# A routed expert layer on six PSUM banks instead of three, with its evictions 384 wide, its weight splitting one step apart, and two conversion pieces moved into the delta rule

## The chip, the core and the metric

The kernel runs on one core of one Trainium2 chip. The core has a matrix engine (TensorE, "PE" in the profile; its weight loads are "PEld"), three engines for the work around it (VectorE "DVE", ScalarE "ACT", GpSimd "POOL"), and queues of transfers that SyncE ("SP") and POOL issue. Matmul results land in PSUM, of which this program names eight banks. The metric is the device time of one launch in microseconds; lower is better.

## The reference

Three stages, each feeding the next:

```python
# 1 delta rule: 4 batches x 8 heads, 768 steps, head size 48
for t in range(S):
    y[:, :, t] = q_t @ state
    state = state + beta_t * outer(k_t, v_t - state.T @ k_t)     # k normalised
# 2 experts: 3072 tokens of 384 features, 8 experts of 1024
expert_idx = argmax(normalised(x) @ normalised(expert_emb).T / tau)
out[mask] = gate_w[mask, None] * (maximum(x[mask] @ w1[e], 0) @ w2[e])
# 3 second network, 384 -> 2048 -> 384; its weights arrive as float64
h = maximum(x @ w_in, 0);  return (h * h) @ w_out
```

## The kernel before

**Arithmetic.** The experts and the second network compute each fp32 product in three matmuls on halves of the numbers (`mm3`, L1136 to L1139): high x high, high x low, low x high. So every weight and every activation exists as a high part (a rounded copy, made by ACT) and a low part (the number less its high part, made by DVE, which must read the high part).

**Stages.** First the delta rule, in 24 steps of 32 tokens (s = 0 to 23), on PE, ACT and DVE in turn; then the experts, one after the other (`moe`, the loop over `e`); then the second network in eight blocks of 384 tokens.

**One expert.** The first layer is eight blocks (`fb`) of nine matmuls, each block into one PSUM bank, taken in turn from a list of three (`P1`: SP_1, YP, GP0). A block is evicted three times: ACT writes the high part `hh` with a Relu (L1234, 448 tokens), DVE the low part `hl` (L1235, 448 tokens), and ACT the 64 tokens past 384 once more, unsplit, as `ht` (L1238, into the tile `lb`). Then the rows of the next expert are transposed on three other banks (`PT`: CH0, CH1, SP_0) and split by `split_x` (ACT L966, DVE L967). Then comes the second layer, in parts t = 0, 3, 1, 2 of 128 tokens, of which part 3 is the tail of 64. `by_count` chooses on the device by the real count of tokens: blocks of 448 with a tail, or blocks of 384 without. In these runs experts 0, 3, 6 and 7 are of the first kind ("full"), 1, 2, 4 and 5 of the second ("short"); the evictions are 448 wide for both.

**Work around the matmuls.** Tables inside `run(k)` place it: k = 1 to 8 stands behind the eight blocks, k = 9 to 12 behind the four parts of the second layer. Two kinds are placed so.

`weights(upto)` splits weight pieces of 768 columns, eight for an expert: ACT copies the high part (L576), DVE subtracts for the low part (L579). The first four are this expert's second layer, loaded by `load_w2` into the tiles `hb` and `lb` (L1131). The other four are the next expert's first layer; they come through a ring of three slots, and `fetch` (L609) asks for piece n+2 when piece n is split.

`q64` is the conversion of the second network's float64 weights to float32 on their raw words: 24 pieces of six DVE operations (L1085, L1089, L1103, L1093, L1105, L1097) and an absolute value on ACT, in place (L1094). The buffers `t4k` of the raw words are two; the load of the next piece (L1069) is issued on SP at the start of each piece. The float32 result goes to DRAM (`wscr`), written by POOL. Nineteen of the DVE operations are placed in an expert, fifteen of them behind the second layer's first three parts.

All of an engine's instructions run in the order of the program, so on ACT and DVE a placed operation stands between two evictions, and an eviction waits until the operations ahead of it are done.

## Time and profile before

| quantity | value |
|---|---|
| median of three runs | 955.38 us (950.41, 955.38, 956.13) |
| profiled execution | 947.13 us, of it 945.4 us span |
| mean granted TensorE clock | 0.968 of full |
| busy over the span | PE 874.5 us (92%), DVE 601.5 (64%), ACT 446.6 (47%), POOL 101.4 (11%) |
| delta rule | to 264.90 us, the first expert matmul |
| experts | 264.90 to 529.65 us |
| second network | from 536.62 us |

Busy shares are means over stages with different limits. A row of the timeline gives start, duration, engine, line and operation, tile written <- tiles read, and in brackets how long the engine stood idle ahead of it and what ended that. The ends of matmuls are modelled and overlap, so their cadence is read from start to start. Lines are those of the kernel before.

### The profile page before, as it was taken

How to read it: one execution, taken by the hardware profiler on the slowest of the kernel's cores; microseconds unless marked ns; L12 is line 12 of the kernel's file. 1: busy time of each engine (PE TensorE's matmuls, PEld its weight loads, DVE VectorE, ACT ScalarE, POOL GpSimd, SP SyncE). 2: the span in 40 equal slices, each digit the busy share in tenths (PEclk: the TensorE clock that was granted, in tenths of full speed). 3: DMA queues.
4: the chain of work that ended last, by engine and by line, in shares of the span. 5: the costliest groups of instructions: out<-in, count | busy, mean ns of one | idle time of the engine just before them, and what ended most of it. 6: DMA issues, size and time to landing. Idle time of an engine off the chain costs nothing.

```text
span 945.4 us, 21992 instructions
## 1 busy us (share of the span) xinstructions
PE 874.5 (92%) x8859; PEld 791.9 (84%) x8859; DVE 601.5 (64%) x1478; ACT 446.6 (47%) x1074; POOL 101.4 (11%) x140
## 2 busy tenths in 40 slices
PE   4678889999899988998999899999999999999998
PEld 2456666767688877888887899999999999999998
DVE  6999999997668777777877781616243342526150
ACT  2256777778644554554455571515142333324140
POOL 3002011213102112212211200000000000000000
PEclk7599999999899999999999999999999999999999
DMA  8685876132256676658536640101010202020000
GB/s 332 231 264 201 255 200 185 41 143 81 71 140 202 227 245 212 229 175 285 188 132 235 200 116 30 22 17 34 17 34 11 40 9 42 10 42 1 26 1 25
DMA packets 103551, 117.13 MB, mean 124 GB/s; under 512 B 60339, under 2 KB 82202, under 8 KB 103440
## 3 DMA queue, kind: packets, MB, share of 16 engines
q1 hardware_dynamic: 95056, 88.72, 30.8%
q0 software_dynamic: 8224, 26.87, 7.6%
q8 instruction: 75, 1.23, 0.6%
q14 instruction: 36, 0.29, 0.1%
q10 hardware_dynamic: 160, 0.01, 0.0%
HBM read 83.47 MB, written 32.89 MB: 123 GB/s over the span
## 4 chain that ended last, share of the span: by engine, by line
PE 48%; DVE 4%; issue 3%; DMA 3%; ACT 2%; SPq 0%; POOL 0%; DVEq 0%; ACTq 0%; POOLq 0%
PE gp L1137 6%; PE gp L1138 6%; PE gp L1139 6%; PE xp L1137 4%; PE xp L1138 4%; PE xp L1139 4%; PE sp L1137 3%; PE yp L1138 3%; PE yp L1137 3%; PE sp L1138 3%; PE yp L1139 3%; PE sp L1139 3%; DMA W<-in_moe_w_dram 1%; DMA x<-y,rows 1%; DVE hl L1235 1%
## 5 line engine op out<-in xcount | busy, mean ns | idle before, releaser
L1339 DVE TENSOR_TENSOR t4k<-t2k 128x384 f32<-128x384 f32 x128 | 71.3, 557 | 200.4 <-ACT t2k L1338 197.9
L1137 PE MATMUL xp<-wb,hh 128*128 128x384 f32 x184 | 62.5, 340 | 0.0
L1138 PE MATMUL xp<-wb,hh 128*128 128x384 f32 x184 | 62.2, 338 | 0.0
L1139 PE MATMUL xp<-wb,hl 128*128 128x384 f32 x184 | 62.1, 338 | 0.0
L272 DVE TENSOR_TENSOR TL<-TL,tmp 128x135 f32<-128x135 f32 (+15 forms) x186 | 60.8, 337 | 1.8
L264 DVE TENSOR_TENSOR tmp<-AL,TL 128x135 f32<-128x135 f32 (+15 forms) x186 | 60.6, 337 | 1.6
L1137 PE MATMUL sp<-xh,W 128*128 128x384 f32 (+1 forms) x156 | 53.9, 345 | 6.2 <-ACT lb L1238 6.0
L1283 POOL DMA_INDIRECT x<-y,rows x32 | 37.8, 1181 | 160.6 <-ACT y L1280 91.8
L1138 PE MATMUL sp<-xl,W 128*128 128x384 f32 (+1 forms) x156 | 53.3, 341 | 0.2 <-DVE xl L967 0.2
L1137 PE MATMUL yp<-xh,W 128*128 128x384 f32 (+1 forms) x156 | 53.4, 342 | 0.0
L1138 PE MATMUL yp<-xl,W 128*128 128x384 f32 (+1 forms) x156 | 53.3, 342 | 0.0
L1139 PE MATMUL sp<-xh,W 128*128 128x384 f32 (+1 forms) x156 | 53.3, 342 | 0.0
L1139 PE MATMUL yp<-xh,W 128*128 128x384 f32 (+1 forms) x156 | 53.3, 342 | 0.0
L1137 PE MATMUL gp<-wb,hh 128*128 128x384 f32 x152 | 51.7, 340 | 0.0
L1138 PE MATMUL gp<-wb,hh 128*128 128x384 f32 x152 | 51.3, 338 | 0.0
L1139 PE MATMUL gp<-wb,hl 128*128 128x384 f32 x152 | 51.3, 338 | 0.0
L1137 PE MATMUL gp<-xh,W 128*128 128x384 f32 (+1 forms) x144 | 49.0, 340 | 1.2 <-ACT lb L1238 1.2
L367 ACT ACTIVATE Sb<-sp 48x384 f32<-48x384 f32 x92 | 44.6, 484 | 9.9 <-PE sp L357 8.7
L1139 PE MATMUL gp<-xh,W 128*128 128x384 f32 (+1 forms) x144 | 48.8, 339 | 0.0
L1138 PE MATMUL gp<-xl,W 128*128 128x384 f32 (+1 forms) x144 | 48.8, 339 | 0.0
L1362 ACT ACTIVATE y<-gp 128x384 f32<-128x384 f32 x12 | 5.9, 492 | 84.3 <-PE gp L1139 84.3
L357 PE MATMUL sp<-Wb,kL 128*48 128x96 f32 x736 | 42.4, 259 | 2.3 <-DVE Wb L319 1.1
(328 smaller groups left out, 2433.8 us busy)
## 6 DMA issues: line engine op xcount, KB each, us to landing
hb<-in_moe_w_dram SPq DMA_DIRECT2D x24, 384.0 KB
t4k<-in_moe_w_in_dram SPq DMA_DIRECT2D x12, 512.0 KB
wscr<-t2k POOLq DMA_DIRECT2D x24, 256.0 KB, 4.1
W<-wscr SPq DMA_DIRECT2D x16, 384.0 KB
W<-in_kq_dram SPq DMA_DIRECT2D x11, 512.0 KB
xs<-padrow POOLq DMA_DIRECT2D x8, 693.0 KB, 7.8
W<-in_moe_w_dram SPq DMA_DIRECT2D x14, 384.0 KB
W<-in_kq_dram POOLq DMA_DIRECT2D x9, 512.0 KB, 6.9
```

Of the source, the lines that this page charges most:

```text
L264: V.tensor_tensor(tv[0], AL[:, j, j + 1 :].unsqueeze(1).broadcast_to([128, n, m]), T[:, :n, j : j + 1].broadcast_to([128, n, m]), ALU.mult,)
L272: V.tensor_tensor(T[:, : j + 1, j + 1 :], T[:, : j + 1, j + 1 :], tv[0], ALU.add)
L357: PE.matmul(SP_[hq][64 * par : 64 * par + D, b * 96 : b * 96 + 96], kL2[g][:, i, b * 2 + hq], Wb[hq].rearrange("p b (m r) e -> p b r m e", ...
L367: A.activation(Sb[hq][r : r + D, :, :, par, :], SP_[hq][r : r + D, 0:384].rearrange("p (b m e) -> p b m e", b=4, m=2), AF.Copy,)
L1137: PE.matmul(ps, hs, rh, start=first, stop=False)
L1138: PE.matmul(ps, hs, rl, start=False, stop=False)
L1139: PE.matmul(ps, ls, rh, start=False, stop=last)
L1235: V.scalar_tensor_tensor(hl[:, fb], ps[:, :CAP], 0.0, hh[:, fb].bitcast(F32), ALU.max, ALU.subtract)
L1283: to_x2 = lambda n=n, t=t, y=y, e=e: G.indirect_dma_start(out=x2, out_offset=bass.IndirectOffsetOnAxis(ap=rows_i[:n, t, e : e + 1].bitcast ...
L1339: V.tensor_tensor(s2, r, r, ALU.mult)
L1362: A.activation(y, ps[:, :DM], AF.Copy)
```

## The change

Six edits:

- Blocks 0, 1 and 2 of a first layer go to the banks of `PT`, blocks 3 to 7 take the three of `P1` in turn. The banks of `PT` are also those of `split_x`.
- `hh` and `hl` are 384 wide. `ht` is evicted on ACT directly behind `hh`, and `hl` on DVE behind both.
- `weights` issues only the high part; the low part is put on a list (`behind`) and issued by `flush`, at the next call of `weights` or at named places.
- The tables differ: weight pieces start at k = 1 and the last first-layer piece is split at k = 11, its low part at k = 12. An expert gets 18 conversion operations, with none at k = 1; the last gets 10 instead of 16.
- The absolute value of a conversion is written to a free part of `lb` (a tile that is now kept for the whole stage) and issued one operation earlier, on a step called `power`.
- Two of the 24 conversion pieces (`EARLY`) are converted in the delta rule: loads at s = 14 on SP, two operations ahead of the end of steps 20 to 23 (between the evictions Ub and Wb), and two, one and one behind them at s = 20, 21, 22; their results are written by SP. They use the buffers `GPs` and `Pm` of the delta rule.

```diff
+    def flush():
+        while behind:
+            hi, lo, raw = behind.pop(0)
+            V.tensor_tensor(lo, raw, hi.bitcast(F32), ALU.subtract)
...
     def weights(upto):
         nonlocal nstep
+        flush()
         while nstep < upto:
+            flush()
             fetch(nstep + 2)
             raw = raws.pop(nstep)
             i, c = pieces[nstep][:2]
-            split(wbuf[i], c, raw.shape[1], raw, A, V)
+            hi, lo = [part(wbuf[i], j, c, raw.shape[1]) for j in range(2)]
+            A.activation(hi, raw, AF.Copy)
+            behind.append((hi, lo, raw))
             nstep += 1
...
             U(s)
             fill(s, 0.25)
+            convert((0, 0, 0, 0, 2, 2, 2, 2)[s - NS + 8] if s >= NS - 8 else 0)
...
+            if s in (NS - 4, NS - 3, NS - 2):
+                convert(2 if s == NS - 4 else 1)
             fill(s + 0.65, 0.35)
+            if s == 14:
+                for m in range(EARLY):
+                    fetch64(m)
+                early.extend(o for m in range(EARLY) for o in w64(m))
...
+        def power():
+            V.tensor_scalar(v["ui"], v["ai"], -0x800000, None, ALU.bitwise_and)
+            A.activation(v["b"], v["h"], AF.Abs)
+
         def low():
-            V.scalar_tensor_tensor(u, v["l"].bitcast(U32), 2.0**-52, u, ALU.mult, ALU.mult)
-            A.activation(v["h"].bitcast(F32), v["h"], AF.Abs)
+            V.scalar_tensor_tensor(v["u"], v["l"].bitcast(U32), 2.0**-52, v["u"], ALU.mult, ALU.mult)
...
-                    weights(8 * e + ((0, 1, 2, 2, 3, 3, 4, 4, 5, 7, 8, 8), (0, 1, 2, 2, 3, 3, 4, 5, 6, 8, 10, 11))[last][k - 1])
-                n = (0, 0, 0, 0, 0, 0, 0, 0, 5, 5, 4, 0) if e == 0 else (1, 0, 0, 1, 0, 1, 0, 1, 5, 5, 5, 0)
+                    weights(8 * e + (1, 1, 2, 3, 4, 4, 5, 5, 6, 7, 8, 8)[k - 1])
+                n = (0, 0, 0, 0, 0, 0, 0, 0, 5, 5, 4, 0) if e == 0 else (0, 1, 0, 0, 0, 1, 0, 1, 5, 5, 5, 0)
                 if last:
-                    n = (2, 1, 0, 2, 0, 2, 0, 2, 4, 3, 0, 0)
+                    n = (0, 1, 0, 0, 0, 1, 0, 1, 3, 4, 0, 0)
...
-            hh = mp.tile([128, 8, CAP], F32R, name="hh", bufs=1)
-            hl = mp.tile([128, 8, CAP], F32R, name="hl", bufs=1)
+            hh = mp.tile([128, 8, 384], F32R, name="hh", bufs=1)
+            hl = mp.tile([128, 8, 384], F32R, name="hl", bufs=1)
...
-                ps = bank(P1)
+                ps = PT[fb] if fb < KD else bank(P1)
...
-                A.activation(hh[:, fb], ps[:, :CAP], AF.Relu)
+                A.activation(hh[:, fb], ps[:, :384], AF.Relu)
+                A.activation(ht[:, fb], ps[:, 384:CAP], AF.Relu)
                 V.scalar_tensor_tensor(
-                    hl[:, fb], ps[:, :CAP], 0.0, hh[:, fb].bitcast(F32), ALU.max, ALU.subtract
+                    hl[:, fb], ps[:, :384], 0.0, hh[:, fb].bitcast(F32), ALU.max, ALU.subtract
                 )
-                A.activation(ht[:, fb], ps[:, 384:CAP], AF.Relu)
```

What this does to the order of instructions is shown at three places, with each instruction's line, operation, tiles and the semaphores that it waits for. The first is ACT at the start of expert 5's first layer, before (`sp`, `yp`, `gp` are the banks of P1, `wb` the weights being split, `lb` the tile of `ht`):

```order
L1234 ACTIVATE hh<-sp_105 128x448 [waits PE_49]
L1238 ACTIVATE lb<-sp_105 128x64 [waits DVE_49]
L1234 ACTIVATE hh<-yp 128x448 [waits PE_49]
L1176 UNCONDITIONAL_BRANCH
L1238 ACTIVATE lb<-yp 128x64 [waits DVE_49]
L576 ACTIVATE wb_4723<-hb 128x768 [waits DMAHW1_49]
L1176 UNCONDITIONAL_BRANCH
L1234 ACTIVATE hh<-gp_107 128x448 [waits PE_49]
L1238 ACTIVATE lb<-gp_107 128x64 [waits DVE_49]
L576 ACTIVATE wb_4723<-hb 128x768 [waits DMAHW2_49]
```

And ACT at the same place after the change (`ch` and `sp_104` are the banks of PT):

```order
L1257 ACTIVATE hh<-ch_102 128x384 [waits PE_49]
L1258 ACTIVATE lb<-ch_102 128x64
L620 ACTIVATE wb_4745<-hb 128x768 [waits DMAHW5_49]
L1197 UNCONDITIONAL_BRANCH x4
L1257 ACTIVATE hh<-ch_103 128x384 [waits PE_49]
L1258 ACTIVATE lb<-ch_103 128x64
L1118 ACTIVATE lb<-t4k 128x512 [waits DMAHW4_49,DMAHW3_49,DVE_49]
L1257 ACTIVATE hh<-sp_104 128x384 [waits PE_49]
L1258 ACTIVATE lb<-sp_104 128x64
L620 ACTIVATE wb_4745<-hb 128x768 [waits DMAHW6_49]
```

`lb` waited for DVE and now waits for nothing of its own; the first weight piece (`wb<-hb`) has moved up by one block.

The second is DVE from the end of expert 4's second layer into expert 5's first, before (L1085 to L1105 are conversion operations, L579 the low part of expert 5's last first-layer piece):

```order
L1085 TENSOR_SCALAR W<-t4k 128x512 [waits DMAHW5_49,DMAHW4_49]
L579 TENSOR_TENSOR wb_4724<-W,wb_4722 128x768 [waits DMAHW6_49,Activation_49]
L1089 SCALAR_TENSOR_TENSOR t2k<-t4k,W 128x512 [waits DMASW5_49,DVE_49]
L1176 UNCONDITIONAL_BRANCH
L1103 TENSOR_SCALAR W<-t2k 128x512 [waits DVE_49]
L1093 SCALAR_TENSOR_TENSOR W<-t4k,W 128x512 [waits DVE_49]
L1105 TENSOR_TENSOR t2k<-t2k,W 128x512 [waits DVE_49]
L1097 SCALAR_TENSOR_TENSOR t2k<-t4k,t2k 128x512 [waits DVE_49,Activation_49]
L1235 SCALAR_TENSOR_TENSOR hl<-sp_105,hh 128x448 [waits Activation_49]
L1085 TENSOR_SCALAR W<-t4k 128x512 [waits DMAHW7_49,DMAHW0_49]
```

After (there the conversion operations are L1109 to L1128, the low part L578, `hl` L1259):

```order
L578 TENSOR_TENSOR wb_4746<-W,wb_4744 128x768 [waits DMAHW4_49,DMAHW3_49,Activation_49]
L1122 SCALAR_TENSOR_TENSOR W<-t4k,W 128x512 [waits DVE_49]
L1197 UNCONDITIONAL_BRANCH x2
L1128 TENSOR_TENSOR t2k<-t2k,W 128x512 [waits DVE_49]
L1125 SCALAR_TENSOR_TENSOR t2k<-lb,t2k 128x512 [waits DVE_49,Activation_49]
L1109 TENSOR_SCALAR W<-t4k 128x512 [waits DMAHW4_49,DMAHW3_49]
L1113 SCALAR_TENSOR_TENSOR t2k<-t4k,W 128x512 [waits DMASW6_49,DVE_49]
L578 TENSOR_TENSOR wb_4746<-W,wb_4744 128x768 [waits DMAHW0_49,Activation_49]
L1197 UNCONDITIONAL_BRANCH x4
L1259 SCALAR_TENSOR_TENSOR hl<-ch_102,hh 128x384 [waits PE_49,Activation_49]
L1259 SCALAR_TENSOR_TENSOR hl<-ch_103,hh 128x384 [waits PE_49,Activation_49]
L578 TENSOR_TENSOR wb_4747<-hb,wb_4745 128x768 [waits DMAHW5_49]
```

The low part of that last piece stood ahead of five conversion operations and now stands behind them; `hl` waits for ACT as before, and for PE by its own semaphore too.

The third is ACT in step 22 of the delta rule, before:

```order
L329 ACTIVATE Ub_111<-ch_103 32x4x48 [waits DVE_49,PE_49]
L329 ACTIVATE Ub_111<-ch_103 32x4x48 [waits Activation_49] x3
L414 ACTIVATE xT<-xp 128x384 [waits DVE_49,PE_49]
L351 ACTIVATE Wb_112<-ch_102 32x4x48 [waits DVE_49,PE_49]
L351 ACTIVATE Wb_112<-ch_102 32x4x48 [waits Activation_49] x3
L420 ACTIVATE junk,XG<-XG 128x384 [waits Activation_49]
```

And after:

```order
L329 ACTIVATE Ub_111<-ch_103 32x4x48 [waits DVE_49,PE_49]
L329 ACTIVATE Ub_111<-ch_103 32x4x48 [waits Activation_49] x3
L1118 ACTIVATE GPs<-GPs 128x512 [waits DMAHW7_49,DMAHW4_49,DVE_49]
L414 ACTIVATE xT<-xp 128x384 [waits PE_49]
L351 ACTIVATE Wb_112<-ch_102 32x4x48 [waits PE_49,Activation_49]
L351 ACTIVATE Wb_112<-ch_102 32x4x48 [waits Activation_49] x3
L420 ACTIVATE junk,XG<-XG 128x384 [waits Activation_49]
```

One of the two moved absolute values (L1118, on the buffer `GPs`) now stands between the last Ub eviction and xT.

## Rows read from the trace of the kernel before

**Rows 1.** The page: its first line.

```profile
span 945.4 us, 21992 instructions
```

**Rows 2.** Windows: stretch, length, busy (x count) per engine, PEclk, DMA share, GB/s.

```profile
298.48:314.89 16.41, 13.74 (x73) 12.43 (x73) 10.59 (x17) 8.48 (x18) 2.75 (x3) 1.00 0.74 262
428.32:445.95 17.63, 14.56 (x73) 14.05 (x73) 13.45 (x22) 7.91 (x17) 3.52 (x4) 0.90 0.89 318
sum 119.41, PE 102.56 PEld 92.85 DVE 88.00 ACT 57.34 POOL 23.48; mean PE 14.65 PEld 13.26 DVE 12.57 ACT 8.19 POOL 3.35
...
600.00:700.00 100.00, 100.00 (x572) 100.00 (x571) 38.28 (x76) 33.22 (x74) 0.00 (x0) 1.00 0.11 25
437.00:441.00 4.00, 4.00 (x16) 4.00 (x15) 1.96 (x4) 2.50 (x6) 1.07 (x1) 0.58 1.05 399
```

**Rows 3.** Timeline of PE: first layers of experts 3, 4 and 5.

```profile
379.34 0.37 PE L1137 MATMUL yp<-xh,wb 128*128 128x448 f32 x1
380.98 0.36 PE L1139 MATMUL yp<-xh,wb 128*128 128x448 f32 x1
...
398.87 0.34 PE L1137 MATMUL sp<-xh,W 128*128 128x384 f32 x1
403.45 0.34 PE L1139 MATMUL gp<-xh,W 128*128 128x384 f32 x1
...
436.30 0.44 PE L1137 MATMUL sp<-xh,wb 128*128 128x384 f32 x1 [3.07 <-ACT lb L1238]
```

**Rows 4.** Waits: engine, line, awaited; us in all, times, longest.

```profile
PE sp L1137 <- ACT lb L1238: 14.5, 11, 3.1
...
ACT lb L1238 <- DVE hl L1235: 70.5, 64, 3.5
```

**Rows 5.** Timelines of ACT and DVE: two blocks of expert 4's first layer.

```profile
407.38 0.22 ACT L1238 ACTIVATE lb<-gp 128x64 f32<-128x64 f32 x1 [1.13 <-DVE hl L1235]
...
408.36 0.96 DVE L579 TENSOR_TENSOR W<-hb,W 128x768 fp32r<-128x768 f32 x1 [1.02 <-ACT W L576]
409.24 0.62 DVE L1235 SCALAR_TENSOR_TENSOR hl<-sp,hh 128x448 fp32r<-128x448 f32 x1
```

**Rows 6.** Timelines of ACT and DVE: expert 5's first layer begins at 428.32.

```profile
430.25 0.85 ACT L576 ACTIVATE wb<-W 128x768 fp32r<-128x768 f32 x1 [3.44 <-DMA W<-in_moe_w_dram]
...
431.13 0.96 DVE L579 TENSOR_TENSOR wb<-W,wb 128x768 fp32r<-128x768 f32 x1 [0.21 <-ACT wb L576]
434.77 0.69 DVE L1097 SCALAR_TENSOR_TENSOR t2k<-t4k,t2k 128x512 f32<-128x512 f32 x1
```

**Rows 7.** Windows, columns as in rows 2: expert 4's second layer; then DVE's run-on.

```profile
413.44:428.32 14.88, 14.88 (x87) 14.17 (x85) 11.75 (x19) 8.88 (x17) 3.06 (x3) 1.00 0.32 96
413.44:435.46 22.02, 19.79 (x113) 18.76 (x111) 18.30 (x30) 11.30 (x21) 4.83 (x5) 1.00 0.43 138
```

**Rows 8.** Timelines of ACT and SP in expert 1's first layer.

```profile
302.99 1.42 SPq L1131 DMA_DIRECT2D hb<-in_moe_w_dram  x3
...
306.09 0.85 ACT L576 ACTIVATE wb<-hb 128x768 fp32r<-128x768 f32 x1
```

**Rows 9.** Lines of 282 to 513 us: count | busy, mean ns | idle before, releaser.

```profile
L1089 DVE SCALAR_TENSOR_TENSOR t2k<-t4k,W 128x512 int32<-128x512 int32 x23 | 15.8, 689 | 0.5
L1085 DVE TENSOR_SCALAR W<-t4k 128x512 int32<-128x512 int32 x23 | 9.7, 420 | 0.0
...
L1094 ACT ACTIVATE t4k<-t4k 128x512 f32<-128x512 int32 x22 | 14.9, 677 | 32.9 <-DVE t2k L1089 20.7 <-issue 12.2
```

**Rows 10.** Timelines: step 22 of the delta rule; the first expert matmuls.

```profile
240.92 1.36 ACT L329 ACTIVATE Ub<-ch 32x192 f32<-32x192 f32 x4 [0.67 <-PE ch L308]
242.69 1.34 ACT L351 ACTIVATE Wb<-ch 32x192 f32<-32x192 f32 x4
...
243.08 0.96 DVE L319 TENSOR_TENSOR Wb<-ch,blk 128x768 f32<-128x768 f32 x1 [1.46 <-ACT Wb L351]
...
265.56 0.47 PE L1138 MATMUL sp<-W 128*128 128x448 f32 x1 [0.19 <-DVE W L967]
```

More of the change, by code (lines that the diff above doesn't have):

```diff
@@ L565 @@
     stg = None
+    spare, early = [], deque()
     raw1 = {}
@@ L571, in part @@
         return wt[2 * i + c // 3072][:, c % 3072 : c % 3072 + n]
-    def split(wt, c, n, raw, Eh, El):
-        hi = part(wt, 0, c, n)
-        if Eh is A:
-            A.activation(hi, raw, AF.Copy)
-        else:
-            Eh.tensor_copy(hi, raw)
-        El.tensor_tensor(part(wt, 1, c, n), raw, hi.bitcast(F32), ALU.subtract)
-    raws, pieces, nstep = {}, [], 0
+    def flush():
+        while behind:
+            hi, lo, raw = behind.pop(0)
+            V.tensor_tensor(lo, raw, hi.bitcast(F32), ALU.subtract)
+    raws, pieces, behind, nstep = {}, [], [], 0
     def cut(w, c, n):
@@ L701, in fill, with convert @@
                 budget = 0.0
+        def convert(n):
+            for _ in range(n):
+                if early:
+                    early.popleft()()
         def due(g):
@@ L998, in overflow @@
                     b1 = mp.tile([128, 2304], F32, name="hb")
-                    b2 = mp.tile([128, 2304], F32, name="lb")
+                    b2 = spare[0]
                     w, xg = b1[:, :1536], b1[:, 1536 : 1536 + ROW]
@@ L1061 @@
     pieces64 = [(i, c) for i in range(2) for c in range(12)]
+    EARLY = 2
     def fetch64(m):
@@ L1066, in fetch64 @@
             src = (moe2_w_in, moe2_w_out)[i].bitcast(I32).rearrange("(a p) f -> p a f", p=128)
-            raw64[m] = stg.tile([128, 1024], I32, name="t4k", bufs=2)
+            if m < EARLY:
+                raw64[m] = gp.tile([128, 4, 8, C], F32, name="GPs", bufs=2).rearrange("p s h j -> p (s h j)").bitcast(I32)
+            else:
+                raw64[m] = stg.tile([128, 1024], I32, name="t4k", bufs=2)
             for o, view in cut(src, c * 1024, 1024):
@@ L1074, in w64 @@
         n = 512
-        u = ring[0][:, 2304 : 2304 + n]
-        ui = u.bitcast(I32)
         v = {}
         def begin():
-            fetch64(m + 1)
             raw = raw64.pop(m)
             v["h"], v["l"] = raw[:, 1::2], raw[:, 0::2]
-            v["a"] = stg.tile([128, 512], F32, name="t2k", bufs=3)[:, :n]
-            v["ai"] = v["a"].bitcast(I32)
-            V.tensor_scalar(ui, v["h"], 3, 0x3FFFFFF8, ALU.logical_shift_left, ALU.bitwise_and)
+            if m < EARLY:
+                a = gp.tile([128, 4, 4, 2, C], F32, name="Pm", bufs=2).rearrange("p f s c j -> p (f s c j)")
+                v["a"], v["u"], v["b"] = a[:, :n], a[:, n:], v["h"].bitcast(F32)
+            else:
+                fetch64(m + 1)
+                v["a"] = stg.tile([128, 512], F32, name="t2k", bufs=3)[:, :n]
+                v["u"], v["b"] = ring[0][:, 2304 : 2304 + n], spare[0][:, 1792:]
@@ L1091, in low @@
         def low():
-            V.scalar_tensor_tensor(u, v["l"].bitcast(U32), 2.0**-52, u, ALU.mult, ALU.mult)
-            A.activation(v["h"].bitcast(F32), v["h"], AF.Abs)
+            V.scalar_tensor_tensor(v["u"], v["l"].bitcast(U32), 2.0**-52, v["u"], ALU.mult, ALU.mult)
         def end():
-            V.scalar_tensor_tensor(v["a"], v["h"].bitcast(F32), float(0x38100000), v["a"], ALU.is_ge, ALU.mult)
-            nc.gpsimd.dma_start(wscr[i][:, c * n : (c + 1) * n], v["a"])
-        return [
-            begin,
-            top,
-            lambda: V.tensor_scalar(ui, v["ai"], -0x800000, None, ALU.bitwise_and),
-            low,
-            lambda: V.tensor_tensor(v["a"], v["a"], u, ALU.add),
-            end,
-        ]
+            V.scalar_tensor_tensor(v["a"], v["b"], float(0x38100000), v["a"], ALU.is_ge, ALU.mult)
@@ L1109, in moe @@
+            (nc.sync if m < EARLY else G).dma_start(wscr[i][:, c * n : (c + 1) * n], v["a"])
+        return [begin, top, power, low, lambda: V.tensor_tensor(v["a"], v["a"], v["u"], ALU.add), end]
     def moe():
@@ L1118, in load_x @@
             load_rows(xe[e], e, False)
-        w2raw, spare = {}, [None]
+        w2raw = {}
+        spare.append(mp.tile([128, 2304], F32, name="lb"))
         def load_w2(e):
@@ L1126, in load_w2 @@
             for nm, a, n in (("hb", 0, 6), ("lb", 6, 2)):
-                t = mp.tile([128, 2304], F32, name=nm)
-                spare[0] = t
+                t = mp.tile([128, 2304], F32, name=nm) if nm == "hb" else spare[0]
                 w2raw[e] += [t[:, i * DM : (i + 1) * DM] for i in range(n)]
@@ L1245, in moe @@
                 fetch(5)
-                q64.extend(o for m in range(len(pieces64)) for o in w64(m))
-                fetch64(0)
+                q64.extend(o for m in range(EARLY, len(pieces64)) for o in w64(m))
+                fetch64(EARLY)
             if e + 1 < E:
@@ L1251, in moe @@
                     load_x(e + 2)
+            flush()
             for i, t in enumerate((0, 3, 1, 2)):
@@ L1352, in moe @@
             part2()
+            flush()
             for t in range(NB):
```

7 lines of the change are left out of this document (6 added, 1 removed).

## The prediction

> **What bounds the kernel now.** The page gives a span of 945.4 us [rows 1] in an execution of 947.13 us. I read the windows first. In the second network PE is busy for the whole of a 100 us window at full clock [rows 2]: nothing that the change touches can help there. The experts are different. The seven first layers of experts 1 to 7 together last 119.41 us (the sum of their windows, from the first matmul to the first transpose) and PE is busy for 102.56 of them [rows 2]. Busy shares flatter PE, so I price the same work by its cadence. In undisturbed stretches of the timeline the start of a matmul follows the last by (380.98 - 379.34)/8 = 0.205 us at 448 columns, and by (403.45 - 398.87)/26 = 0.176 us at 384 [rows 3]. Three full experts have 3 x 72 = 216 matmuls of the first kind, four short ones 288 of the second: 44.3 + 50.7 = 95.0 us. So 119.4 - 95.0 = **24.4 us are lost** in seven first layers. That is all that the rebuilt first layers can give back.
>
> The waits say what PE stands for: blocks start late because ACT's `lb` eviction (L1238) has not freed the bank, 14.5 us in eleven waits on bank SP_1 alone. ACT in turn waited 70.5 us, 64 times, for DVE's `hl` [rows 4]. The timeline shows this lockstep: `lb` at 407.38 had waited 1.13 us for `hl`; then ACT splits a weight piece, DVE's low part (0.96 us) has to wait 1.02 us for it, and the next `hl` ends at 409.24 + 0.62 = 409.86 [rows 5]. One block with a weight piece takes some 2.5 us, against 9 x 0.176 = 1.59 us of matmuls. Three banks cannot cover that for long.
>
> The second cause is a late start. Expert 5's first layer begins at 428.32 [rows 2]. ACT gets its last weight piece at 430.25, after 3.44 us of waiting for the transfer; DVE's low part is at 431.13, and DVE is done with its conversion at 434.77 + 0.69 = 435.46, 7.1 us into the layer [rows 6]. Only then comes the first `hl`, and PE stands for 3.07 us until 436.30 [rows 3]. From 437 to 441 the granted clock is 0.58 [rows 2], that is, most of the stretch is at 1.2 GHz instead of 2.4; at full clock those 4 us would have been some 1.7 us shorter.
>
> **The change, part by part.**
>
> *Six banks.* Blocks 0 to 5 of a layer now need no eviction of the same layer. The first block that can wait is block 6, at 6 x 9 x 0.176 = 9.5 us in a short layer, 11.1 in a full one. DVE may be 7 us late, as in expert 5, and then has only 2.4 us to bring block 3's `hl` out, but the tables also take the lag away (below).
>
> *Lockstep.* `hl` no longer holds ACT up: `ht` needs only the matmuls. The 70.5 us of ACT's waits [rows 4] lose their cause, and ACT runs ahead. The low part is issued behind the next eviction, so the 1.02 us that DVE waited for ACT [rows 5] is covered by that eviction. The 384 wide parts are shorter by 64/448 of the columns; I count nothing for them, since DVE's time is hidden once six banks cover it.
>
> *The start of a layer.* The last conversion operation used to end up to 7.1 us into the layer. From the end of expert 4's first layer to that operation, DVE was busy 18.30 of 22.02 us [rows 7]. The change takes out of this the leftovers of the first layer (one conversion operation 0.68, one `hl` 0.62, a low part 0.96, a rest of another `hl`, about 0.35) and one more low part, 0.96, which now stands earlier: 18.3 - 3.6 = 14.7. With the idle 3.7 us, or 2.7 without the lockstep's share, DVE ends 17.4 to 18.4 us after the first layer's end. But the low part of the last piece now stands behind the five conversion operations, not ahead of them. Its first reader is the third matmul of block 2's last chunk, which starts 403.45 - 398.87 = 4.6 us into the layer [rows 3]; with 14.88 us of second layer [rows 7] that is 19.5 us after the first layer's end. A margin of 1.1 to 2.1 us. I leave 3.0 us of loss in experts 2 to 7 (0.5 each), between nothing (the margin holds) and 14 (first rival).
>
> *Expert 1 keeps a loss.* Its second layer's weights are asked for at 302.99 and reach ACT at 306.09 [rows 8]; the change does nothing to that load. The piece now stands one block earlier on ACT, ahead of block 1's eviction. Behind it come three `hh`, two `ht`, another piece and block 3's `hl`: 306.09 + 0.85 + 3 x 0.62 + 2 x 0.22 + 0.85 + 0.62 = 310.7 with 0.62 for an eviction of 448 [rows 5, 8]; at 384 I take 310.6. Block 6 wants that bank at 298.48 + 9.5 = 308.0 [rows 2]: 2.6 us stay of what expert 1 loses.
>
> *Conversion.* Taking one operation from each of seven experts and moving 12 of them saves DVE 0.42 to 0.69 us apiece [rows 9]; its worth is within the margin above. In the delta rule, two operations (0.42 + 0.69 = 1.11 us) fit in DVE's 1.46 us of idle time ahead of Wb [rows 10], so I cost them at nothing; without that cover they cost up to 12 x 0.69 = 8.3 us. The absolute value does cost: in step 22 ACT runs from Ub (240.92 + 1.36 = 242.28) almost straight to Wb at 242.69, and Wb is what DVE waits for [rows 10]. An operation of 0.68 us [rows 9] goes between: **+0.7**, bounds 0 and 1.4 (both pieces). The out-of-place absolute value frees a raw buffer earlier, so loads are issued earlier; that works against waits like the 3.44 us above, and is counted in the same 3.0.
>
> *Expert 0's start.* Block 0 now writes a bank whose transposed rows DVE has just read. PE waits 0.19 us for such a read already at 265.56 [rows 10]: **+0.2**, bounds 0 and 0.7.
>
> *Sum.* 24.4 - 2.6 - 3.0 = 18.8 gained, 0.9 paid: 17.9. The profiled execution goes from 947.1 to 929.2. It lies 8.3 us under the median of the runs shown, so the median goes from 955.4 to **937.5**.
>
> **Rivals.**
>
> *R1: the last low part, or its transfer, is the new wait.* If DVE is as late as before, the low part ends 7.1 + 0.96 us into expert 5's layer, where 4.6 is wanted: 3.5 us. Half that as a mean over seven experts is some 2 us each, 14 in all, in place of the 2.6 and the 3.0: 24.4 - 14 - 0.9 = 9.5, median **945.9**. For it: the margin is an estimate from one expert, and the 3.44 us wait for a transfer shows that ACT can be held [rows 6]. Against: 3.6 us of work leave that stretch.
>
> *R2: readers of one bank stay in series.* `hl` now stands behind `hh` and `ht`, and the order's rows show it waiting for ACT. If DVE is held by ACT's two reads of a bank, each block costs DVE a further `ht`, 0.22 us [rows 5]: 8 x 0.22 x 4 short experts, whose margin is the smallest, is 7.0 us. Gain 10.9, median **944.5**. Against: ACT, freed of waiting, runs ahead, so the read is over before DVE comes.
>
> The Trainium skill, page "PSUM — Partial Sum Buffer", section "PSUM bank collisions raise a hardware error", says that two engines may not touch the same bank and the same quadrant of partitions at once, reads against reads included. By that rule the eviction of a bank stays serial whatever the order of the code. The trace agrees so far: `lb` waited for `hl`, 64 times, though it needs nothing that `hl` writes.
>
> *R3: slower.* The same low part becomes later than 3.5 us beyond the need (8.1 us into the layer) in all seven experts: 24.4/7 = 3.5 eats the whole gain, and from there it is a loss. Each such wait is longer than the 3.07 us after which the clock fell [rows 3], and would bring its own slow stretch of some 1.7 us [rows 2]: 7 x 1.7 + 0.9 = 12.8, median **968.2**. Against: it needs in every expert a lag that before only expert 5 had.
>
> *R4: nothing unblocks,* since weights and not evictions set the pace: +0.9, median **956.3**. Against: PE's waits name the eviction.
>
> **How the numbers follow.** The forecast (gains of 14 to 24 us) has 0.58, R1 0.22, R2 0.10, R4 0.05, R3 0.05. About 1% is what a measurement of this kernel can tell from no change: faster is under 945.8, slower over 964.9. Faster: 0.57 of the forecast, half of R1 (its time lies on the bound), 0.06 of R2: 0.74. Slower: R3, 0.05. The rest, 0.21, is the same. Bounds: with no loss left in experts 2 to 7 the median is 934.5; the runs scatter by 5.7 us, mostly downwards of the median, so the low end is 929. The high end, 949, takes in R1 with 3 us on top. The likeliest case alone: 931 to 941.
>
> **What would show it.** The seven windows should shrink from 119.4 to about 100.6 us, with PE's clock at 1.00 in all. PE's waits for the eviction should be nearly gone except in expert 1, near block 6; new waits of PE on DVE's L578 at block 2 mean R1; `hl` waiting for L1258 with PE waiting for `hl` means R2. ACT's waits for `hl` must be gone. The delta rule should end 0.7 us later than 264.9; if by several, the moved operations had no cover. The forecast is wrong if the windows stay above 110 us, or if time lost to banks comes back as waits for weights.

## The result, and the profile after

The changed kernel takes 927.11 us in the median (923.03 to 931.18, four runs), against 953.46 us for the kernel before in the same comparison: a ratio of 0.9725 with an interval of 0.9669 to 0.978. Three later comparisons gave 0.9743 (0.9711 to 0.9774), 0.9742 (0.9701 to 0.9784) and 0.9721 (0.9687 to 0.9755). The medians differ by 26.4, 24.8, 24.6 and 25.6 us. The forecast was a gain of 17.9 us and a time of 937.5 us, with a range from 929.0: right in sign, 7 to 8.5 us too small, and the time lies 1.9 us under the range and 10.4 us under the forecast. Of these 10.4 us, 1.9 are the kernel before, whose median is 953.46 us here and was 955.38 us in the three runs that the forecast had.

The profiled execution took 926.72 us.

```profile
span 925.0 us, 22005 instructions
```

The windows of the seven first layers (columns as in rows 2; expert 1, expert 5 and the sum of all seven) answer to those of before:

```profile
300.71:317.52 16.81, 13.44 (x73) 12.48 (x73) 11.30 (x18) 9.29 (x23) 2.81 (x3) 1.00 0.74 259
...
419.84:432.51 12.67, 12.67 (x73) 12.64 (x73) 11.26 (x19) 8.82 (x21) 3.37 (x3) 1.00 0.93 325
...
sum 98.88, PE 95.51 PEld 90.86 DVE 76.15 ACT 62.79 POOL 20.66; mean PE 13.64 PEld 12.98 DVE 10.88 ACT 8.97 POOL 2.95
```

From 119.41 to 98.88 us. The six layers of experts 2 to 7 lose nothing any more: each short one takes 12.67 or 12.68 us and each full one 14.67 or 14.69, which is 72 times 0.176 and 0.204 us, the cadence of rows 3, and PE is busy throughout at full clock. Only expert 1 still loses, 4 us in this execution. The waits (engine, line, awaited; us in all, times, longest) say where:

```profile
DVE hl L1259 <- ACT lb L1258: 28.7, 37, 2.6
...
PE sp L1158 <- ACT wb L620: 2.0, 1, 2.0
PE ch L1160 <- DVE wb L578: 1.4, 1, 1.4
```

PE's waits for the eviction [rows 4] are gone but for one in expert 1, and ACT's 70.5 us of waits for `hl` are gone too. What is left on PE in these layers is two waits in expert 1. DVE now waits for ACT's `ht`, 37 times, as the rival R2 said, but in experts 2 to 7 PE doesn't stand for it.

DVE's timeline at the start of expert 5's first layer (419.84), and a row of ACT's there, answer to rows 6:

```profile
422.45 0.95 DVE L578 TENSOR_TENSOR wb<-W,wb 128x768 fp32r<-128x768 f32 x1
423.32 0.55 DVE L1259 SCALAR_TENSOR_TENSOR hl<-ch,hh 128x384 fp32r<-128x384 f32 x1
...
427.01 0.56 DVE L1259 SCALAR_TENSOR_TENSOR hl<-sp,hh 128x384 fp32r<-128x384 f32 x1 [0.58 <-ACT lb L1258]
...
426.38 0.49 ACT L1257 ACTIVATE hh<-sp 128x384 fp32r<-128x384 f32 x1 [0.25 <-PE sp L1160]
```

The last low part ends at 422.45 + 0.95 = 423.40, 3.6 us into the layer, where 4.6 is the latest that PE can take: a margin of 1.0 us. The first `hl` starts 3.5 us into the layer here. By block 3 the evictions have caught up: ACT waits 0.25 us for PE to finish the block, and DVE 0.58 us for ACT. Before, DVE was busy with its conversion until 7.1.

Expert 1 is as forecast in place, not in size. PE's, DVE's and ACT's timelines:

```profile
303.64 0.44 PE L1160 MATMUL ch<-xh,wb 128*128 128x384 f32 x1 [1.36 <-DVE wb L578]
...
314.28 0.42 PE L1158 MATMUL sp<-xh,wb 128*128 128x384 f32 x1 [2.01 <-ACT wb L620]
```

```profile
302.63 0.96 DVE L578 TENSOR_TENSOR wb<-W,wb 128x768 fp32r<-128x768 f32 x1 [1.41 <-ACT y L1304]
...
305.97 0.95 DVE L578 TENSOR_TENSOR wb<-W,wb 128x768 fp32r<-128x768 f32 x1
```

```profile
308.63 0.85 ACT L620 ACTIVATE wb<-hb 128x768 fp32r<-128x768 f32 x1 [3.90 <-DMA hb<-in_moe_w_dram]
...
312.20 0.84 ACT L620 ACTIVATE wb<-hb 128x768 fp32r<-128x768 f32 x1 [1.19 <-DMA hb<-in_moe_w_dram]
```

The wait at block 6 (2.01 us of idle, forecast 2.6) is there: the weight piece holds ACT for 3.90 us, and the next one for 1.19. A second wait, 1.36 us, is for a low part, but not for the one that R1 named. It stands at block 0's ninth matmul, the first reader of the third piece's low part, which DVE starts at 302.63; the last piece's follows at 305.97, and PE doesn't wait for it. The change put the third piece's low part behind five conversion operations and behind the branch that follows `run(10)` in expert 0 (`overflow`, L992), where DVE stood idle for 0.9 to 1.4 us in the four profiles. In the three later profiles this layer took 15.9, 14.4 and 15.1 us.

In the delta rule the absolute value stands where the forecast put it, on ACT's way from Ub to Wb in step 22:

```profile
242.91 1.36 ACT L329 ACTIVATE Ub<-ch 32x192 f32<-32x192 f32 x4 [0.72 <-PE ch L308]
244.41 0.68 ACT L1118 ACTIVATE GPs<-GPs 128x512 f32<-128x512 int32 x1
...
245.50 1.34 ACT L351 ACTIVATE Wb<-ch 32x192 f32<-32x192 f32 x4
```

From the end of Ub to Wb: 245.50 - 244.27 = 1.23 us, before 242.69 - 242.28 = 0.41 [rows 10]. It costs 0.8.

### The profile page after: what moved, and what is told of

It is laid out like the page before. It is cut to its first block, busy times and chain, and to the rows that moved or that the text cites. A ratio compares the mean times of both kernels' runs of the same rounds, so it can differ in the third digit from the quotient of the medians.

```text
span 925.0 us, 22005 instructions
## 1 busy us (share of the span) xinstructions
PE 868.9 (94%) x8859; PEld 792.9 (86%) x8859; DVE 592.3 (64%) x1478; ACT 443.2 (48%) x1074; POOL 104.0 (11%) x138
## 3 DMA queue, kind: packets, MB, share of 16 engines
q8 instruction: 75, 1.23, 0.6%
## 4 chain that ended last, share of the span: by engine, by line
PE 65%; DMA 1%; ACT 0%; another core or an unknown queue 0%; DVE 0%; SPq 0%; issue 0%; ACTq 0%
PE gp L1158 8%; PE gp L1159 8%; PE gp L1160 8%; PE xp L1158 5%; PE xp L1160 5%; PE xp L1159 5%; PE sp L1159 4%; PE sp L1158 4%; PE sp L1160 4%; PE yp L1159 3%; PE yp L1160 3%; PE yp L1158 3%; PE gp L1284 1%; PE ch L981 1%; PE ch L1158 1%; PE ch L1159 1%
## 5 line engine op out<-in xcount | busy, mean ns | idle before, releaser
L1160 PE MATMUL yp<-xh,W 128*128 128x384 f32 (+1 forms) x147 | 49.8, 339 | 0.0
L1159 PE MATMUL yp<-xl,W 128*128 128x384 f32 (+1 forms) x147 | 49.8, 339 | 0.0
L1158 PE MATMUL yp<-xh,W 128*128 128x384 f32 (+1 forms) x147 | 49.8, 339 | 0.0
L1160 PE MATMUL gp<-xh,W 128*128 128x384 f32 (+1 forms) x135 | 45.7, 339 | 0.0
L1158 PE MATMUL gp<-xh,W 128*128 128x384 f32 (+1 forms) x135 | 45.7, 338 | 0.0
L1159 PE MATMUL gp<-xl,W 128*128 128x384 f32 (+1 forms) x135 | 45.7, 338 | 0.0
L1388 ACT ACTIVATE y<-xp 128x384 f32<-128x384 f32 x12 | 5.9, 492 | 81.6 <-PE xp L1160 81.6
```

The source lines that it names most:

```text
L1158: PE.matmul(ps, hs, rh, start=first, stop=False)
L1159: PE.matmul(ps, hs, rl, start=False, stop=False)
L1160: PE.matmul(ps, ls, rh, start=False, stop=last)
L1388: A.activation(y, ps[:, :DM], AF.Copy)
```

## The experiments

The window sums below are those of the seven first layers of experts 1 to 7, each from one profiled execution of its kernel. They do not hold the scatter of the delta rule, and two profiles of one kernel differ by 0.3 to 2.5 us in them, the changed kernel's by its expert 1 alone.

| kernel | first layers, us | ratio to before (interval) |
|---|---|---|
| before, twice | 119.4, 119.7 | 1 |
| before + six banks | 124.6 | 1.004 (1.0019 to 1.0061) |
| before + `ht` ahead of `hl` | 114.2 | 0.990 (0.987 to 0.993) |
| before + low parts a step later | 107.5 | 0.9875 (0.9811 to 0.9938) |
| before + both reorderings, twice | 99.5, 100.1 | 0.9784 (0.9726 to 0.9843), 0.9745 (0.971 to 0.978) |
| changed, four profiles | 98.9, 98.0, 96.4, 97.1 | 0.9721 to 0.9743 |
| changed, three banks | 97.4 | 0.974 (0.9703 to 0.9778) |
| changed, `hl` ahead of `ht` | 102.5 | 0.9814 (0.9758 to 0.987) |
| changed, low parts at once | 100.0 | 0.9747 (0.9693 to 0.9801) |
| changed, no pieces in the delta rule | 100.1 | 0.9761 (0.9707 to 0.9815) |
| changed, old weight table | 96.2 | 0.9738 (0.9703 to 0.9774) |
| changed, with repairs | 96.3 | 0.9719 (0.9677 to 0.9761) |
| changed, with repairs and three banks | 96.7 | 0.9716 (0.9685 to 0.9747) |

**The kernel before, again.**

> The kernel before, unchanged, for a second profile of it. Its profiled execution was 947.13 us while its other runs were 950.4 to 956.1. If the forecast's step from that profile to the median (8.3 us carried over as a constant) was the miss, another execution spans 949 to 955 us and the extra time stands in the seven first layers (119.41 us in the profile read), as more waits for evictions. If it is a constant around the span, the span is again near 945.4 us.

951.89 us median of ten runs, ratio 0.9981 (0.9958 to 1.0004); its profiled execution spans 943.9 us, again far below its median. The first layers sum to 119.66 us, so the loss in them is the same in both profiles. What differs between executions is the time ahead of them. On ACT's timelines, step 23's Wb eviction starts at 250.32 and 250.36 us in the two profiles of before, at 254.14 with six banks and 254.12 with `ht` ahead, all with the same delta rule code. The ends of the spread are two more kernels with that code, before + low parts a step later, and before + both reorderings in its second profile:

```profile
258.70 1.31 ACT L351 ACTIVATE Wb<-ch 32x192 f32<-32x192 f32 x4
```

```profile
249.00 1.30 ACT L351 ACTIVATE Wb<-ch 32x192 f32<-32x192 f32 x4
```

Nearly ten microseconds apart. The spread was already there at step 19 (229.31 and 220.01), ahead of all operations that the change adds to these steps; before had 220.97 and 221.33. Both profiles of before stand near the fast end.

**The changed kernel, again (three times).**

> The changed kernel, unchanged, for the ratio with more rounds and a second profile. Ratio 0.970 to 0.978; first layers of experts 2 to 7 again without a gap (82.1 us in all), expert 1 near 16.8 us. The span should scatter by less than before, since PE waits for little.

927.83 us, ratio 0.9743; 82.1 us for experts 2 to 7, no gap, as expected; expert 1 took 15.9 us, not 16.8.

> The changed kernel unchanged, beside the repaired one on the same chip. Again 0.971 to 0.978 of the kernel before; first layers of experts 1 to 7 in 98 to 99 us.

928.52 us, ratio 0.9742. The sum was 96.4, lower than expected, by expert 1 alone (14.4 us).

> The changed kernel, unchanged, as the measure for the other three of this call: 0.972 to 0.977 of the kernel before.

927.15 us, ratio 0.9721.

**Six banks alone.**

```diff
-                ps = bank(P1)
+                ps = PT[fb] if fb < KD else bank(P1)
```

> The kernel before with six banks for the first layers and nothing else. Theory banks (three banks were too few, as the forecast had it): at least 12 us faster, ratio 0.987 or less. Theory lag (DVE comes 4 to 7 us late into a layer and then evicts one block in 1.35 or 2.5 us, whatever the banks): hl of block 3 comes 10 to 14 us into the layer, block 6 wants it at 9.5 to 11.1, so most of the loss stays: 0 to 6 us faster, ratio 0.994 to 1.000.

956.37 us, ratio 1.004: slower by 0.4%, which neither theory had. In expert 2 PE now runs six blocks and then waits once, for long (timelines of PE and DVE, a window, and the sum of the seven first layers):

```profile
349.98 0.69 PE L1137 MATMUL sp<-xh,W 128*128 128x384 f32 x1 [5.21 <-ACT lb L1238]
```

```profile
346.54 0.62 DVE L1235 SCALAR_TENSOR_TENSOR hl<-sp,hh 128x448 fp32r<-128x448 f32 x1
349.06 0.62 DVE L1235 SCALAR_TENSOR_TENSOR hl<-sp,hh 128x448 fp32r<-128x448 f32 x1
```

```profile
350.00:353.00 3.00, 3.00 (x10) 3.00 (x11) 1.85 (x4) 1.75 (x4) 0.00 (x0) 0.52 0.00 0
...
sum 124.55, PE 102.86 PEld 96.64 DVE 91.52 ACT 60.18 POOL 23.93; mean PE 14.69 PEld 13.81 DVE 13.07 ACT 8.60 POOL 3.42
```

The `hl` of block 3 still comes 14 us into the layer (349.06 - 335.11), 2.5 us after that of block 2. PE waits 5.21 us for it, and then runs at a granted clock of 0.52, near 1.2 GHz, for the next 3 us. The evictions set the pace; more banks only move the waiting to the end of this layer. In all it even grows: PE's idle time in the seven layers (their length less PE's busy time) is 21.7 us, against 16.9 before. The clock is below full in four of the seven layers (0.82 to 0.91), before in two (0.90 and 0.91). How much of the 5 us is the clock's was not separated.

**Three banks in the changed kernel.**

```diff
-                ps = PT[fb] if fb < KD else bank(P1)
+                ps = bank(P1)
```

> The changed kernel with three banks for the first layers, all else kept. Theory banks: 8 to 14 us slower than the changed kernel. Theory lag: DVE's first hl ends 2.7 us into the layers of experts 2 to 7, block 3 wants the bank at 4.8, and later blocks have it in time too; only expert 1 loses, 1 to 3 us, and expert 0 starts some 0.7 us earlier: within 3 us of the changed kernel.

929.47 us, ratio 0.974. Expert 2's window and the sum:

```profile
336.68:349.36 12.68, 12.68 (x74) 12.64 (x74) 11.28 (x19) 8.82 (x21) 3.66 (x3) 1.00 0.89 323
...
sum 97.44, PE 95.80 PEld 90.86 DVE 76.25 ACT 62.16 POOL 20.76; mean PE 13.69 PEld 12.98 DVE 10.89 ACT 8.88 POOL 2.97
```

Experts 2 to 7 lose nothing with three banks either; expert 1 takes 15.4 us. So the theory of the banks, on which the forecast's first step stood, fails from both sides: six banks alone gain nothing, and the changed kernel does not need them.

**`ht` ahead of `hl` alone.**

```diff
+                A.activation(ht[:, fb], ps[:, 384:CAP], AF.Relu)
                 V.scalar_tensor_tensor(
                     hl[:, fb], ps[:, :CAP], 0.0, hh[:, fb].bitcast(F32), ALU.max, ALU.subtract
                 )
-                A.activation(ht[:, fb], ps[:, 384:CAP], AF.Relu)
```

> The kernel before with ht issued ahead of hl, nothing else: ACT no longer waits for DVE in a block. Theory lockstep (this wait is the first cause; once ACT runs ahead, the high parts of weights are also ready when DVE comes): the seven first layers go from 119.5 us to 100 to 107, 10 to 18 us faster. Theory weights (DVE's waits for the high parts set the pace, ht is only a passenger): at most 5 us faster, first layers above 114 us.

944.32 us, ratio 0.990, first layers 114.2: 5.3 us less in the layers, which is the second theory's result. The medians differ by 8.8 us, more than it allowed; the stages of this one profile do not show where the other 3.5 are. The sum of the windows, and the waits:

```profile
sum 114.21, PE 100.97 PEld 94.75 DVE 95.79 ACT 66.54 POOL 24.50; mean PE 14.42 PEld 13.54 DVE 13.68 ACT 9.51 POOL 3.50
...
DVE W L579 <- ACT W L576: 21.9, 12, 4.2
DVE wb L579 <- ACT wb L576: 18.8, 8, 4.4
PE sp L1137 <- DVE hl L1236: 11.4, 5, 2.9
```

ACT's 70 us of waits are gone. But DVE waits as long as before for the high parts of weights, 40.7 us in 20 waits, where the kernel before had 41.7 in 43:

```profile
DVE W L579 <- ACT W L576: 22.3, 22, 1.9
...
DVE wb L579 <- ACT wb L576: 19.4, 21, 1.4
```

DVE comes nearly as late into a layer (first `hl` at 6.4 to 7.4 us in experts 2, 3, 5 and 6, before 6.2 to 7.3).

**Low parts a step later, alone.** `split` puts the low part on a list, and `flush` issues it, as in the change.

> The kernel before with the low parts of the weights issued one step later, and nothing else. Theory lag: DVE's waits for ACT's high parts (34.8 us in experts 1 to 7) mostly go, some 4 us an expert, DVE starts its evictions 2 to 4 us into a layer instead of 4 to 7: 8 to 16 us faster. Theory banks: 0 to 4 us faster.

941.83 us, ratio 0.9875, first layers 107.5, inside the expectation of the theory of DVE's lag. The sum and the waits:

```profile
sum 107.46, PE 101.17 PEld 89.67 DVE 77.83 ACT 57.30 POOL 22.03; mean PE 14.45 PEld 12.81 DVE 11.12 ACT 8.19 POOL 3.15
...
ACT lb L1246 <- DVE hl L1243: 65.9, 64, 3.9
DVE hl L1243 <- ACT hh L1242: 41.8, 38, 2.2
```

DVE no longer waits for weights at all; the first `hl` comes 2.6 to 5.7 us into a layer instead of 3.8 to 7.3. But the 41.7 us have moved: DVE now waits 41.8 us for `hh`, which ACT can only write after `ht`, which waits for the last `hl`. The lockstep keeps 8 us of loss in these layers (107.5 against the 99.5 of the next run, which removes it too).

**Both, and nothing else.** Three banks, 448 wide, the old tables, no piece in the delta rule.

> The kernel before with ht ahead of hl and the low parts a step later; three banks, 448 wide, the old tables, no piece in the delta rule. Theory order (the order of four instructions makes the gain): first layers 98 to 102 us, 16 to 22 us faster than before, so that banks, widths, tables and moved pieces are worth 1 to 4 us together. If tables and moved pieces are needed too: first layers above 105 us.

931.72 us, ratio 0.9784; first layers 99.5. Of the long waits between the two engines one stays:

```profile
DVE hl L1244 <- ACT lb L1243: 22.2, 30, 3.4
```

and the windows sum to:

```profile
sum 99.53, PE 96.77 PEld 90.69 DVE 83.95 ACT 62.26 POOL 20.36; mean PE 13.82 PEld 12.96 DVE 11.99 ACT 8.89 POOL 2.91
```

20 of the 21 or 22 us, from the order of two instructions and a delay of one step. Apart they give 5.3 and 12.1 us in this sum, 17.4 if they simply added up, and together 20.

> The kernel before with only the two reorderings (ht ahead of hl, low parts a step later), beside the changed kernel on one chip. If the other four edits are worth nothing that can be told, both ratios agree within 0.2%. If they are worth what the stages of one profile show (first layers 99.5 against 96.4 to 98.9 us), it is 1 to 4 us slower than the changed kernel.

927.58 us, ratio 0.9745, beside 0.9721 for the changed kernel. In the comparison before, the ratios were 0.9784 and 0.9742. The intervals overlap both times. The four other edits together are worth 2 to 4 us by these ratios, and 2.2 by the first layers (99.8 against 97.6 in the mean); the times do not tell that from nothing.

**The changed kernel with `hl` ahead of `ht`.** The two statements of the eviction are exchanged, the reverse of the edit above.

> The changed kernel with hl issued ahead of ht, the order of the kernel before, all else kept; ACT then waits for DVE in each block. Theory lockstep: 6 us or more slower than the changed kernel. Theory lag: from a first hl at 2.1 us, hl of block 3 ends near 8.7 us and block 6 wants it at 9.5: within 2 us of the changed kernel. If the two engines could read one bank together, ACT's ht would not wait for hl.

936.68 us, ratio 0.9814: some 7 us slower than the changed kernel by the ratios (0.9814 - 0.9743, the latter from another comparison), 4.9 by the first layers (97.6 in the mean of four). By the times that is what the theory of lockstep expected, by the layers it lies between the two. The waits and the sum:

```profile
ACT lb L1261 <- DVE hl L1258: 54.1, 64, 3.6
DVE hl L1258 <- ACT hh L1257: 45.9, 43, 3.4
...
PE sp L1158 <- ACT lb L1261: 4.6, 3, 3.1
```

```profile
sum 102.47, PE 97.66 PEld 92.08 DVE 70.42 ACT 55.21 POOL 20.46; mean PE 13.95 PEld 13.15 DVE 10.06 ACT 7.89 POOL 2.92
```

`ht` needs nothing that `hl` writes, and waits for it 64 times; with `ht` first, `hl` waits for `ht`. The reader of a bank that comes second in the program waits for the first.

The Trainium skill, page "PSUM — Partial Sum Buffer", section "PSUM bank collisions raise a hardware error", has it that two engines may not read one bank in the same quadrant of partitions at once. The trace agrees so far as both orders show the second reader waiting; the waits are in the program, so no run here shows what the hardware would do without them.

**The changed kernel with low parts at once.**

```diff
             behind.append((hi, lo, raw))
+            flush()
```

> The changed kernel with each low part issued directly behind its high part, all else kept. Theory lag: DVE stands some 1 us at each of eight pieces of an expert again; the margin at the last piece (it ends 3.6 us into a layer, 4.6 is wanted) and the evictions give way: 6 to 15 us slower than the changed kernel. Theory banks: six banks cover it, 0 to 3 us slower.

929.07 us, ratio 0.9747; first layers 100.0, 2 to 3 us more than the changed kernel's mean (97.6). DVE waits again, nearly as long as before:

```profile
DVE W L578 <- ACT W L620: 20.0, 14, 4.3
DVE wb L578 <- ACT wb L620: 17.5, 12, 4.3
```

and the first `hl` comes 5.9 to 6.8 us into the layers of experts 2, 3, 5 and 6. It costs little: with `ht` ahead, fewer operations and six banks, the late evictions catch up. So the theory that DVE's wait for weights is decisive in itself is wrong too; on the kernel before, beside `ht` ahead, the delay of the low part is worth 114.2 - 99.5 = 14.7 us, and here 2.4. That is what the theory of the banks expected of this run (0 to 3 us). So six banks may be what covers for late evictions here, though the changed kernel as it stands does not need them. The same kernel with three banks would tell, and was not run; nor were the narrower evictions tried alone.

**No pieces in the delta rule.** `EARLY` is 0, and the conversion table that of before.

> The changed kernel with no conversion piece in the delta rule: 19 conversion operations an expert and 16 in the last, by the table of the kernel before. The delta rule should end some 0.9 us earlier; the end of the experts should get back its wait for the one-hot rows (0.9 us) and the wait for the read-back (1.6 us): 1 to 3 us slower in all. If the moved pieces are what makes room on DVE, 6 us or more slower, with gaps in the first layers of experts 2 to 7.

929.83 us, ratio 0.9761. The first layers of experts 2 to 7 lose 2.4 us, all in expert 2, where PE waits for an eviction behind a weight piece (window of that layer; PE's timeline):

```profile
334.43:349.46 15.03, 13.15 (x74) 12.54 (x73) 10.38 (x18) 8.49 (x21) 3.44 (x5) 1.00 0.86 283
```

```profile
345.86 0.41 PE L1158 MATMUL sp<-xh,W 128*128 128x384 f32 x1 [1.77 <-ACT W L620]
```

The end of the experts does not get its waits back, against the expectation: from expert 7's last first-layer matmul to the second network it is 20.4 us here and 20.9 in the changed kernel, against 23.9 and 22.9 before. The two reorderings alone have 20.4 and 20.6, so this gain too is theirs. The time is 1.7 to 3.8 us above the changed kernel's by the ratios (0.9721 to 0.9743 in other comparisons), which the intervals do not separate.

**The old weight table.** `(0, 1, 2, 2, 3, 3, 4, 4, 5, 7, 8, 8)` and the old row of the last expert.

> The changed kernel with the old table of weight pieces (0, 1, 2, 2, 3, 3, 4, 4, 5, 7, 8, 8), all else kept. Theory order (the reorderings make the gain): within 2 us of the changed kernel, expert 1 perhaps shorter, since its first piece stands a block later. Theory tables: 5 us or more slower, with gaps at block 2 or 3 of the layers of experts 2 to 7.

927.89 us, ratio 0.9738, first layers 96.2: the theory of order. The new table is worth nothing that can be seen; expert 1 was shorter with the old one (13.8 us, against 14.4 to 16.8).

**Repairs.** The changed kernel with expert 1's first weight piece three blocks later, expert 0's last low part ahead of four conversion operations, and expert 0's first blocks on P1; then the same with three banks throughout.

```diff
+                    weights(8 * e + ((0, 0, 0, 1, 2, 3, 4, 4, 5, 7, 8, 8) if e == 1 else (1, 1, 2, 3, 4, 4, 5, 5, 6, 7, 8, 8))[k - 1])
...
+                if e == 0 and k == 11:
+                    flush()
...
-                ps = PT[fb] if fb < KD else bank(P1)
+                ps = PT[fb % KD] if fb // KD == (e == 0) else bank(P1)
```

> The changed kernel with three small repairs: expert 1 splits its second layer's weights from the fourth block on (they reach ACT 7.6 to 7.9 us into the layer); expert 0's last first-layer piece gets its low part ahead of four conversion operations; expert 0's blocks begin on the banks of P1. Expert 1's first layer from 15.9 or 16.8 us to 12.7 to 13.2, the start some 0.7 us earlier: 3 to 5 us faster than the changed kernel. If the transfers of expert 1's weights are the limit whatever the order, its layer stays above 14.5 us and the gain is under 2 us.

> The repaired kernel (a later table for expert 1, a prompt low part at the end of expert 0) with three banks throughout. If six banks are worth nothing once evictions come in time, first layers of experts 1 to 7 are again 96 to 98 us and the time is that of the repaired kernel, 0.970 to 0.975 of the kernel before, 0 to 4 us under the changed one. If expert 1 needs the banks, its layer is 2 us or more longer than 14.1.

926.1 us, ratio 0.9719 (0.9677 to 0.9761), against 0.9742 for the changed kernel in the same comparison; with three banks 925.98 us, 0.9716 (0.9685 to 0.9747), against 0.9721. The lowest medians measured, and not told from the changed kernel. Expected were 3 to 5 us and a layer of 12.7 to 13.2 us for expert 1; it takes 14.1. Expert 1's windows, of the repaired kernel and of that with three banks:

```profile
304.10:318.23 14.13, 13.03 (x74) 12.60 (x73) 10.36 (x18) 9.17 (x21) 2.62 (x3) 1.00 0.72 246
```

```profile
304.23:318.43 14.20, 13.26 (x74) 12.53 (x73) 10.35 (x18) 8.84 (x21) 2.57 (x3) 1.00 0.70 239
```

The wait at block 6 is gone; that at block 0 stays (PE's and DVE's timelines of the repaired kernel):

```profile
306.77 0.45 PE L1160 MATMUL ch<-xh,wb 128*128 128x384 f32 x1 [1.10 <-DVE wb L578]
```

```profile
305.75 1.82 DVE L578 TENSOR_TENSOR wb<-W,wb 128x768 fp32r<-128x768 f32 x2 [1.29 <-DVEq L992]
```

The repair at the end of expert 0 moved the wrong low part. The last one now stands directly behind the third (x2), but PE waits for the third, and that one still stands behind the same conversion operations and the branch at L992, where DVE is idle for 1.29 us. Putting it ahead of that branch was not tried.

## Why the prediction was right in sign and short in size

**In short.** The forecast was too high by 10.4 us, and four of its steps failed. In the mechanism, six banks were to cover the late evictions; alone they cost time, and the changed kernel is as fast without them. In the sum, the 3.0 us of loss left in experts 2 to 7 measured 0, and the end of the experts, which had no term, gained some 2 us. And 8.3 us were carried from the profile to the median as if they were the same for both kernels; the kernel after shows 0.4.

**The loss of 24.4 us** was read rightly: without it the layers of experts 2 to 7 take just the cadence's time, and both profiles of before have the same sum.

**Six banks: this step failed.** The forecast took them as the cover that makes late evictions harmless, and counted 6 x 9 x 0.176 = 9.5 us of grace. Alone they lose 5 us in the first layers, and with three banks the changed kernel is as fast (0.974 and 0.9743 in one comparison). Such a grace helps only if the evictions are fast enough on average; at 2.5 us for a block with a weight piece against 1.59 of matmuls those of the kernel before were not. The forecast had both numbers in its first part, said of three banks that they cannot cover this for long, and did not ask the same of six. This error did not show in its sum, since the two reorderings give back what it had credited to the banks: on this point the size came out by luck, in part.

**Lockstep and low parts: right, but not weighed.** Both mechanisms are as described, and in the kernel before they are nearly the whole gain in these layers: 114.2 and 107.5 alone, 99.5 together. In the changed kernel taking the first back costs 4.9 us and the second 2.4. The forecast treated them as one edit among six and never asked what each was worth without the others.

**The start of a layer: right in place, and a term mis-sized.** DVE's low part ends 3.6 us into a layer, 4.6 is wanted; the forecast's margin was 1.1 to 2.1, the measured one 1.0. The 3.0 us that were left for experts 2 to 7 did not come: a term of 3.0 that measured 0.

**Expert 1: right in place.** Forecast 2.6 us; the layer takes 16.8, 15.9, 14.4 and 15.1 us in four profiles where 12.7 would do, so 4.1, 3.2, 1.7 and 2.4, in the mean 2.9. That sum holds a wait that the forecast did not have, up to 1.4 us at block 0 for the low part of the third piece. R1's own wait, for the last low part at block 2, did not appear in any of the four profiles.

**The end of the experts: not foreseen.** From expert 7's last first-layer matmul to the second network, 23.9 and 22.9 us before, 20.8 to 21.0 after, and the second network itself 0.4 to 0.8 longer; its second matmul waits 0.63 us for DVE, before 0.15 and 0.48. Together some 2 us of gain. PE's timelines before and after:

```profile
529.65 0.58 PE L942 MATMUL ch<-t2k,t4k 128*128 128x384 f32 x2 [0.87 <-DVE t2k L1312]
...
533.50 1.16 PE L952 MATMUL ch<-ident,xe 128*128 128x128 f32 x8 [0.94 <-DMA xe<-x]
```

```profile
515.38 0.45 PE L1158 MATMUL sp<-xh,W 128*128 128x384 f32 x1 [0.80 <-ACT xh L982]
516.46 0.44 PE L1159 MATMUL sp<-xl,W 128*128 128x384 f32 x1 [0.63 <-DVE xl L983]
```

The forecast looked at PE's waits in the first layers only. Here PE waited 0.87 us for DVE and, in this profile, 1.6 us in two waits for rows read back; after the change these waits are gone. That DVE's lag was behind both is likely and not shown: each reordering alone leaves 23.8 and 23.9 us.

**Expert 0: right.** Its first matmul starts later (0.86 us of idle, on DVE's read), and its layer is then 14.7 us instead of 15.5: nothing in sum, where 0.2 of loss was forecast. In one of the four profiles it took 16.6 us, so this is not sharp.

**The delta rule.** The absolute value costs 0.8 us where 0.7 was forecast. From Wb of step 19 to Wb of step 23 seven profiles of before and its variants take 28.9 to 29.6 us, mean 29.3; ten with the moved pieces take 29.7 to 32.6, mean 30.4. That is 1.1 us, within the bounds; but the changed kernel without moved pieces took 30.1 in its one profile, so not all of it is certain.

**Summing up by stages:** first layers 21.9 (119.55 to a mean of 97.6), expert 0 nothing, the end 2, less 1.1: some 23 us, where the forecast had 17.9. **The step to the median** was the other miss. The profile of before lay 8.3 us under the median, and the forecast moved both by the same amount, as if 8.3 us belonged to every execution of either kernel. They do not: the profiled execution after lies 0.4 us under its median, and that of before 6.3 under the median of four. That step is 7.9 of the 10.4 us by which the median was missed; the other 2.5 are the profile's own, 926.7 us against 929.2. The profile after gained less than its stages, 20.4 us, since its step 19 stood 1.9 us later (222.89 against 220.97). Both profiles of before caught a short delta rule (step 19 at 220.97 and 221.33, all others 220.01 to 229.31), so a single profile doesn't tell the median within some 5 us. The medians differ by 24.6 to 26.4 us; the last 2 to 3 us between these and the sum over stages are inside the intervals and were not placed.

R2's mechanism is seen, 28.7 us of waiting, at no cost in experts 2 to 7, whose layers take just the cadence's time. At block 3 of expert 5 both engines wait for PE's block, ACT 0.25 us and DVE behind it 0.58. R3 and R4 are ruled out. One count in the forecast was off and changed no term: experts 1 to 6 give up one conversion operation each and the last expert six, not one in each of seven.

## What to carry to other kernels

Where two engines work in turns on the same buffer, look for the waits that only the order makes: a reader placed behind another reader whose result it does not need, a subtraction directly behind the copy that it does need. Set the time of a full turn of that chain (here 2.5 us with a weight piece) against the time of the engine that fills the buffer (1.59 us) before adding buffers; where the turn was longer, six buffers only gathered the waits. Try such edits alone and together: the worth of each alone (5.3 and 12.1 us) did not give that of the pair (20).
